# Token mixing's first layer: four groups of 112 tokens, or three of 128 and a rest of 64

## The chip, the cores and the metric

The kernel runs on one core of one Trainium2 chip. The metric is the device time of one execution in microseconds (us), as the median of several runs. The engines have short names below: PE is TensorE (its matmuls; PEld its weight loads), DVE is VectorE, ACT is ScalarE, POOL is GpSimd, and SP is SyncE, which here only issues DMAs.

## The reference

Attention with normalised queries and keys over 8 batches, 12 heads, 448 tokens and 64 columns a head; then an MLP mixer on the heads side by side, 448 tokens by 768 channels. All is float32, and the four mixer weights arrive as float64.

```python
q_n, k_n = rmsnorm(q, g_q), rmsnorm(k, g_k)
attn = softmax(q_n @ k_n.T / 8)
x = (attn @ v), heads side by side             # (8, 448, 768)
xt = x.transpose(0, 2, 1)                       # (8, 768, 448)
h = maximum(xt @ w_tok1, 0) @ w_tok2            # w_tok1 (448, 256), w_tok2 (256, 448)
u = x + h.transpose(0, 2, 1)
h2 = maximum(u @ w_ch1, 0) @ w_ch2              # w_ch1 (768, 1536), w_ch2 (1536, 768)
out = u + h2
```

What changes is the product `xt @ w_tok1`: a contraction over 448 tokens into 256 outputs, for each of 768 channels.

## The kernel before, in words

**Order of the work.** The program is one list of items per batch, which the code makes by hand: `merge` weaves lists by their given costs, `run` emits them, and `later` puts off an item (a DMA, mostly) by a number of these costed microseconds. Each engine then runs its own instructions in the order of emission. All engines but SP are scheduled by hand, and nearly all DMAs go through SP's one queue. [...]

**Attention** keeps `uT`, the attention's result with channels on partitions and tokens along the row, six tiles of 128 channels a batch. Its matmuls (`score`, L381; `values`, L454; `ones`, L434) work on 64 rows and 64 columns each, four of them on the four quarters of the array. The attention of batch b+1 is placed between the mixer's products of batch b. Queries and keys come by L1253 (`loads`), are squared on ACT (L1272), summed on DVE (L1286), folded on ACT (L1294) and made into roots from L1303 on.

**Token mixing's first layer** (`tok1`, L749) needs the tokens on partitions, so `uT` is turned first. In batch 0, `trans_x` does it with PE: four transposes a tile into one PSUM tile (L733), which ACT copies to `x` (L735). In later batches DVE transposes blocks of 32 (L741) into `xt`, four DMAs write that to DRAM (`send_x`, L709), and one DMA reads it back as `x` (`load_x`, L716): 112 partitions, each with three channel tiles by four token groups of 128 channels. The two halves h of the channels (384 each) are turned and loaded separately. `tok1(b, jc, h)` then does, for output tile jc and half h, four matmuls over groups of 112 tokens (L755) into one bank of `ps_M`, and ACT's Relu (L758) writes `h1`. A batch has four such items, (jc, h) = (0,0), (1,0), (0,1), (1,1). A float32 matmul stands in the trace as two passes.

**What follows it.** `tok2` (L763) contracts `h1` with `w_tok2`, into `ps_M` again, and DVE adds the result to `uT` (L768). `ps_M` has two banks, shared by all mixer products; `ps_S` has four, for scores, transposes and row sums. The channel mixing is a Strassen-like scheme of seven products: `ch1` (L879) and `ch2` (L936), with sums on DVE and POOL (L884, L945 and others), and weights in units that SP loads ahead from DRAM (L810). In batch 0 the natural products are done instead (`first_stage`, L851), while the weights are converted from float64 by DVE and ACT (L268 to L302) from raw loads (L176) and stored (L192). POOL then makes further sums of the weights (L204 to L207), stored by L211 and reloaded by L240, through batches 0 and 1. `trans_y` (L972) and `send_y` (L699) turn and write out the finished tiles.

**Weights of this layer.** `weight_chunks` (L133) loads `w_tok1` as two chunks of 112 rows with two token groups each, into `w1_sb`.

## Time and profile before

| | us |
|---|---|
| median of 3 runs (lowest, highest) | 1310.11 (1308.59, 1312.26) |
| the profiled execution | 1311.39 |
| its span, first to last instruction | 1309.6 |
| L755 MATMUL, 256 passes, busy | 84.5 |
| L763 MATMUL, 192 passes, busy | 78.3 |
| L879 and L936 MATMUL, 3528 passes, busy | 692.8 |
| x loads (L716): 14 DMAs of 672 KB, issue to landing | 6.9 |
| unit loads (L810): 294 DMAs of 384 KB, issue to landing | 4.1 |
| granted TensorE clock, mean | 0.994 |

A line of groups reads: line, engine, operation, tiles written and read, rows and columns of the array, shapes and count; then busy time, mean of one, and the engine's idle time ahead of it. Matmuls overlap, so a group's busy time says more than count times mean, and the spacing of starts says most. In a timeline or a chain the first number is the start from the beginning of the span, the second the length. A "q" behind an engine's name is its sequencer: it waits, or issues a DMA.

### The profile page before, as it was taken

What the parts mean: (1) busy time and instruction counts of PE and PEld (TensorE: products, weight loads), DVE (VectorE), ACT (ScalarE), POOL (GpSimd) and SP (SyncE); (2) the same over time, 40 slices, a digit from 0 to 9 for tenths busy, and PEclk for the clock granted to TensorE, in tenths of its full rate; (3) what the DMA queues carried; (4) which work ended last, traced back from release to release, by engine and by line L of the source; (5) the groups of instructions that cost most, each with busy time, mean ns of one, the idle gap of its engine ahead of it and who ended that gap; (6) DMA issues with size and microseconds to landing.
All of it is one profiled execution on the core that took longest, in us unless ns stands there. A gap on an engine that the chain in (4) does not pass through costs nothing.

```text
span 1309.6 us, 20269 instructions
## 1 busy us (share of the span) xinstructions
PE 1264.2 (97%) x7408; PEld 930.7 (71%) x7408; DVE 763.4 (58%) x1205; ACT 373.5 (29%) x740; POOL 350.6 (27%) x575
## 2 busy tenths in 40 slices
PE   5998999989998999999999999999999999999996
PEld 3444444447777688796778777796788868797996
DVE  6998768827774466645765366654666266433212
ACT  5652423213331133302441044302332033200100
POOL 1302410447352122221332122321242123111220
PEclk9999999999999999999999999999999999999999
DMA  9667485899979676686649667694757864385554
GB/s 207 171 190 179 122 218 149 196 257 254 246 203 225 146 186 157 156 224 121 163 122 233 141 152 175 157 235 98 169 151 174 204 139 142 117 224 132 172 177 83
DMA packets 502450, 228.07 MB, mean 174 GB/s; under 512 B 374532, under 2 KB 464004, under 8 KB 502340
## 3 DMA queue, kind: packets, MB, share of 16 engines
q1 hardware_dynamic: 489218, 224.83, 68.9%
q10 hardware_dynamic: 12994, 1.84, 0.8%
q8 instruction: 61, 1.00, 0.3%
q14 instruction: 49, 0.40, 0.1%
q0 software_dynamic: 128, 0.00, 0.0%
HBM read 187.07 MB, written 39.52 MB: 173 GB/s over the span
## 4 chain that ended last, share of the span: by engine, by line
PE 79%; DVE 9%; DMA 4%; SPq 3%; issue 2%; ACT 1%; POOL 1%; DVEq 0%; ACTq 0%; POOLq 0%
PE m_ps L936 25%; PE m_ps L879 25%; PE s_ps L381 8%; PE o_ps L454 8%; PE m_ps L763 5%; PE m_ps L755 5%; PE m_ps L851 3%; DVE raw L269 1%; DVE raw L271 1%; PE d_ps L434 1%; DMA qk_t<-in_k_dram 1%; DMA raw<-in_moe_w_ch_dram 1%; DVE stage L302 1%; DVE ms L1286 1%; DMA hb<-in_q_dram 1%
## 5 line engine op out<-in xcount | busy, mean ns | idle before, releaser
L936 PE MATMUL m_ps<-hb,unit 128*128 128x224 f32 x1764 | 339.8, 353 | 4.1 <-DVE uT L945 2.4
L936 PEld LDWEIGHTS m_ps<-hb,unit 128*128 128x128 f32 x1764 | 332.2, 190 | 15.2 <-issue 12.5
L879 PE MATMUL m_ps<-tu,unit 128*128 128x224 f32 x1008 | 201.9, 355 | 0.1
L879 PEld LDWEIGHTS m_ps<-tu,unit 128*128 128x128 f32 x1008 | 189.0, 190 | 14.6 <-issue 9.9
L385 ACT ACTIVATE e<-s_ps 128x448 f32<-128x448 f32 x294 | 138.3, 551 | 205.6 <-PE s_ps L381 197.5
L879 PE MATMUL m_ps<-uT,unit 128*128 128x224 f32 x756 | 151.1, 354 | 0.0
L879 PEld LDWEIGHTS m_ps<-uT,unit 128*128 128x128 f32 x756 | 142.2, 190 | 7.0 <-issue 4.6
L381 PE MATMUL s_ps<-qkT 64*64 64x448 f32 x1260 | 142.2, 545 | 0.4 <-ACT x L735 0.4
L454 PE MATMUL o_ps<-e,v 64*64 64x448 f32 x1148 | 129.1, 538 | 0.2
L422 DVE TENSOR_TENSOR es<-es,e 128x896 f32<-128x896 f32 x90 | 109.7, 1219 | 14.1 <-ACT e L385 8.9
L945 POOL TENSOR_TENSOR uT<-uT,r 128x448 f32<-128x448 f32 (+1 forms) x56 | 56.6, 1020 | 228.3 <-DVE r L945 140.9
L884 DVE TENSOR_TENSOR r<-m_ps,r 128x448 f32<-128x448 f32 x63 | 39.2, 622 | 108.1 <-PE m_ps L879 55.7
L945 DVE TENSOR_TENSOR uT<-uT,m_ps 128x448 f32<-128x448 f32 (+1 forms) x70 | 33.8, 499 | 110.9 <-PE m_ps L936 110.9
L381 PEld LDWEIGHTS s_ps<-qkT 64*64 64x64 f32 x1260 | 44.8, 132 | 67.1 <-issue 59.2
L454 PEld LDWEIGHTS o_ps<-e,v 64*64 64x64 f32 x1148 | 45.2, 133 | 62.4 <-issue 58.0
L884 POOL TENSOR_TENSOR hb<-r,r 128x448 f32<-128x448 f32 x21 | 24.0, 1145 | 235.6 <-ACT r L900 235.6
L763 PE MATMUL m_ps<-w_sb,h 128*128 128x448 f32 x192 | 78.3, 561 | 8.9 <-DVE uT L768 8.9
L755 PE MATMUL m_ps<-x,w_sb 112*128 112x384 f32 x256 | 84.5, 487 | 1.0 <-ACT x L735 1.0
L755 PEld LDWEIGHTS m_ps<-x,w_sb 112*128 112x128 f32 x256 | 48.4, 190 | 34.3 <-ACT x L735 1.3
L763 PEld LDWEIGHTS m_ps<-w_sb,h 128*128 128x128 f32 x192 | 36.5, 195 | 46.8 <-issue 27.8
L885 ACT ACTIVATE hb<-hb 128x448 f32<-128x448 f32 x63 | 36.3, 577 | 116.7 <-DVE hb L884 98.1
L1286 DVE TENSOR_REDUCE ms<-sq 128x28 f32<-128x896 f32 (+2 forms) x44 | 47.5, 1079 | 35.2 <-ACT sq L1272 32.2
(122 smaller groups left out, 1372.8 us busy)
## 6 DMA issues: line engine op xcount, KB each, us to landing
unit<-ws SPq DMA_DIRECT2D x294, 384.0 KB, 4.1
raw<-in_moe_w_ch_dram SPq DMA_DIRECT2D x72, 256.0 KB, 3.6
v<-in_v_dram SPq DMA_DIRECT2D x96, 112.0 KB, 3.7
xs<-xt SPq DMA_DIRECT2D x56, 168.0 KB, 4.7
x<-xs SPq DMA_DIRECT2D x14, 672.0 KB, 6.9
out_dram<-turned SPq DMA_DIRECT2D x168, 56.0 KB, 2.0
qk_t<-in_q_dram SPq DMA_DIRECT2D x144, 56.0 KB, 3.3
qk_t<-in_k_dram SPq DMA_DIRECT2D x144, 56.0 KB, 3.9
```

What stands on the lines that cost most here:

```text
L381: nc.tensor.matmul(out=pss[i][rows_of(i, a), 0:S], lhsT=qkT[h, 1, k * D:(k + 1) * D], rhs=qkT[h, 0, :], start=True, stop=True)
L385: nc.scalar.activation(out=e[:, i, :], in_=pss[i][:, 0:S], func=AF.Exp)
L422: nc.vector.tensor_tensor(out=es[:], in0=(es if k > 1 else st["e", t, 0])[:], in1=st["e", t, k][:], op=ALU.add)
L454: nc.tensor.matmul(out=st["o", p][a * D:(a + 1) * D, 0:S], lhsT=vt[rows, k * D:(k + 1) * D], rhs=e[rows, :], **kw)
L755: nc.tensor.matmul(out=ps[:, 0:HC], lhsT=w1_sb[0:R, c, jc * P:(jc + 1) * P], rhs=st["x", b, h][0:R, :, c, :], start=(c == 0), stop=(c == N ...
L763: nc.tensor.matmul(out=ps[:, 0:S], lhsT=st["h1", jc][:, cc * P:(cc + 1) * P], rhs=w2_sb[:, jc].rearrange("p c r -> p (c r)"), start=(jc == ...
L851: nc.tensor.matmul(out=ps, lhsT=a[:, o + 2 * half, :], rhs=natural(half)[:, :, t, :] if wide else u[:, half * KC + t, :], start=(t == 0 an ...
L879: nc.tensor.matmul(out=ps[:, j * HS:(j + 1) * HS], lhsT=w[:, t, j, :], rhs=m, start=(t == 0), stop=(t == KC - 1))
L884: add = lambda e, o, x, y: e.tensor_tensor(out=o, in0=x, in1=y, op=ALU.add)
L936: nc.tensor.matmul(out=ps[:, j * HS:(j + 1) * HS], lhsT=st["w"](j, t), rhs=hb[:, HB[what], t, :], start=(t == 0), stop=(t == KF - 1))
L945: add = lambda e, o, x, y: e.tensor_tensor(out=o, in0=x, in1=y, op=ALU.add)
L1286: self.nc.vector.tensor_reduce(out=st["ms", p][:, p % 2, lo:hi], in_=sq[:, lo:hi], axis=AX_X, op=ALU.add)
```

## The change

The 448 tokens are taken as three groups of 128 and a rest of 64. The rest is kept twice, on the lower and on the upper 64 partitions, in `x` and in `w1_sb`; the matmul of output tile 0 takes it from the lower half and that of tile 1 from the upper. In batch 0 the rest of a half follows the first tile's three groups. In later batches (`alone`) both output tiles' three groups of half 0 come first, then the four rest matmuls of both halves in one run, then half 1's three groups for each tile; half 0's two sums stay in `ps_M` until then, and half 1's two lie in `ps_S`. The Relu is moved to `tok1_out`. `load_x` issues five DMAs instead of one (three of 128 partitions, two of 64), the second chunk of `w_tok1` three instead of one, and `trans_x` three ACT copies a tile instead of one. The order of everything else on each engine is as before. `NM` is 3 and `D` is 64.

```diff
-        for c in range(0, NS, 2):
-            first.append((R, [w1v[:, c:c + 2, :]], w1_sb[0:R, c:c + 2, :].rearrange("p c n -> p (c n)")))
+        w1v = moe_w_tok1[0:2 * P].rearrange("(c p) n -> p c n", p=P)
+        rest = moe_w_tok1[NM * P:S]
+        for c, srcs in ((0, [w1v]), (2, [moe_w_tok1[2 * P:NM * P], (rest, rest)])):
+            first.append((P, srcs, w1_sb[:, c:c + 2, :].rearrange("p c n -> p (c n)")))
...
     def load_x(b, half):
-        nc.sync.dma_start(
-            out=x_tile(b, half)[0:R].rearrange("p j c n -> p (j c) n"),
-            in_=st.pop("xs")[:].rearrange("(g p) n -> p g n", p=R))
+        x, xs = x_tile(b, half), st.pop("xs")[:].rearrange("(j s) n -> s j n", j=KC)
+        for j in range(KC):
+            nc.sync.dma_start(
+                out=x[:, j, 0:NM, :], in_=xs[0:NM * P, j].rearrange("(c p) n -> p c n", p=P))
+        for a in range(2):
+            nc.sync.dma_start(out=x[a * D:(a + 1) * D, :, NM, :], in_=xs[NM * P:S])
...
-            for c in range(NS):
+            for c in range(NM):
                 nc.tensor.transpose(
-                    ps[0:R, c * P:(c + 1) * P], st["uT", b][:, j, c * R:(c + 1) * R], ident[:, :])
-            nc.scalar.copy(
-                out=st["x", b, half][0:R, o], in_=ps[0:R, :].rearrange("p (c n) -> p c n", c=NS))
+                    ps[:, c * P:(c + 1) * P], st["uT", b][:, j, c * P:(c + 1) * P], ident[:, :])
+            nc.tensor.transpose(ps[0:D, NM * P:NS * P], st["uT", b][:, j, NM * P:S], ident[:, :])
+            x = st["x", b, half]
+            nc.scalar.copy(out=x[:, o, 0:NM], in_=ps[:, 0:NM * P].rearrange("p (c n) -> p c n", c=NM))
+            for a in range(2):
+                nc.scalar.copy(out=x[a * D:(a + 1) * D, o, NM], in_=ps[0:D, NM * P:NS * P])
...
     def tok1(b, jc, h):
-        cs = slice(h * HC, (h + 1) * HC)
-        if h == 0:
-            st["h1", jc] = h1_pool.tile([P, C], F32, name="h1", tag="h1")
-        ps = m_tile()
-        for c in range(NS):
-            nc.tensor.matmul(
-                out=ps[:, 0:HC], lhsT=w1_sb[0:R, c, jc * P:(jc + 1) * P], rhs=st["x", b, h][0:R, :, c, :],
-                start=(c == 0), stop=(c == NS - 1))
-        nc.scalar.activation(out=st["h1", jc][:, cs], in_=ps[:, 0:HC], func=AF.Relu)
+
+        def main(start, stop):
+            for c in range(NM):
+                nc.tensor.matmul(
+                    out=st["t1", h][jc][:, 0:HC], lhsT=w1_sb[:, c, jc * P:(jc + 1) * P],
+                    rhs=st["x", b, h][:, :, c, :], start=start and c == 0, stop=stop and c == NM - 1)
+
+        def rest(h, starts):
+            for i in range(NJ):
+                rows = slice(i * D, (i + 1) * D)
+                nc.tensor.matmul(
+                    out=st["t1", h][i][:, 0:HC], lhsT=w1_sb[rows, NM, i * P:(i + 1) * P],
+                    rhs=st["x", b, h][rows, :, NM, :], start=starts[i], stop=not starts[i])
+
+        alone, first = b > 0 and not shifted, jc == 0
+        if first and not (alone and h):
+            st["t1", h] = [m_tile() for i in range(NJ)]
+        if not alone:
+            main(first, not first)
+            if first:
+                rest(h, (False, True))
+            tok1_out(jc, h)
+            return
+        if h == 0:
+            main(True, False)
+            return
+        if first:
+            st["t1", h] = [s_tile("t1_ps") for i in range(NJ)]
+            rest(0, (False, False))
+            rest(1, (True, True))
+            for i in range(NJ):
+                tok1_out(i, 0)
+        main(False, True)
+        tok1_out(jc, h)
+
+    def tok1_out(jc, h):
+
         if h == 0:
             st["h1", jc] = h1_pool.tile([P, C], F32, name="h1", tag="h1")
+        nc.scalar.activation(
+            out=st["h1", jc][:, h * HC:(h + 1) * HC], in_=st["t1", h][jc][:, 0:HC], func=AF.Relu)
```

More of the change, by code (lines that the diff above doesn't have):

```diff
@@ L73, in whole @@
     assert S == NK * D and NPAIR % 2 == 0 and D % 32 == 0
+    NM = S // P
+    assert S - NM * P == D and NM == NS - 1 and NJ == 2
     UNITS = 8
@@ L135, in weight_chunks @@
         first, second = [], []
-        w1v = moe_w_tok1.rearrange("(c p) n -> p c n", c=NS)
-        for c in range(0, NS, 2):
-            first.append((R, [w1v[:, c:c + 2, :]], w1_sb[0:R, c:c + 2, :].rearrange("p c n -> p (c n)")))
+        w1v = moe_w_tok1[0:2 * P].rearrange("(c p) n -> p c n", p=P)
+        rest = moe_w_tok1[NM * P:S]
+        for c, srcs in ((0, [w1v]), (2, [moe_w_tok1[2 * P:NM * P], (rest, rest)])):
+            first.append((P, srcs, w1_sb[:, c:c + 2, :].rearrange("p c n -> p (c n)")))
         for j in range(NJ):
@@ L154, in columns @@
     def columns(i):
-        src = chunks[i][1][0]
-        return WCOLS if chunks[i][2] is None or len(src.shape) == 3 else src.shape[-1]
+        return WCOLS if chunks[i][2] is None else chunks[i][2].shape[-1]
     def raw_tile():
@@ L171, in weight_load @@
             to = flat[:, k * n:(k + 1) * n]
-            if wide:
-                src = src.bitcast(U32)
-            if len(src.shape) == 3:
-                to = to.rearrange("p (i n) -> p i n", i=src.shape[1])
-            nc.sync.dma_start(out=to, in_=src)
+            for a, part in enumerate(src if isinstance(src, tuple) else (src,)):
+                at = to[a * D:(a + 1) * D] if isinstance(src, tuple) else to
+                if wide:
+                    part = part.bitcast(U32)
+                if len(part.shape) == 3:
+                    at = at.rearrange("p (i n) -> p i n", i=part.shape[1])
+                nc.sync.dma_start(out=at, in_=part)
         st["raw", i] = t
```

## The prediction

> **What bounds the kernel now.** I read the page first. It gives the span and how busy each engine is. The slices of TensorE then say where it is not busy.

> ```profile
> span 1309.6 us, 20269 instructions
> ...
> PE 1264.2 (97%) x7408; PEld 930.7 (71%) x7408; DVE 763.4 (58%) x1205; ACT 373.5 (29%) x740; POOL 350.6 (27%) x575
> ...
> PE   5998999989998999999999999999999999999996
> ```

> TensorE (PE) is the bound, but not everywhere: the digits below 9 lie in the first third. The table by stretch separates the batches (bounds, length, then busy time of PE, PEld, DVE, ACT, POOL, granted clock, DMA share):

> ```profile
> 125.00:265.60 140.60, 136.00 (x541) 63.59 (x540) 107.62 (x173) 45.66 (x82) 36.75 (x60) 0.99 0.71 177
> 265.60:431.70 166.10, 157.14 (x938) 118.50 (x937) 99.88 (x162) 46.18 (x97) 79.27 (x132) 0.99 0.91 237
> 431.70:582.70 151.00, 150.99 (x922) 118.48 (x921) 87.19 (x131) 42.35 (x87) 38.60 (x62) 1.00 0.71 173
> 582.70:733.70 151.00, 150.99 (x922) 118.49 (x921) 87.17 (x131) 42.48 (x87) 38.58 (x62) 1.00 0.69 167
> ```

> From 431.7 us on (batches 2 to 7) PE is busy in 150.99 of 151.00 us: every nanosecond taken from PE there is taken from the end. Batch 1 (265.6 to 431.7) leaves PE idle for 9.0 us, with the DMA engines 91% busy; batch 0 idles too. The waits of PE (total, times, longest) say on what, and the chain that ended last, cut to 170 to 284 us, says what stood behind it:

> ```profile
> PE m_ps L763 <- DVE uT L768: 8.9, 3, 4.8
> ...
> PE m_ps L936 <- DVE uT L945: 2.4, 1, 2.4
> PE m_ps L936 <- DMA unit<-ws: 1.7, 1, 1.7
> ```

> ```profile
> 262.47 0.80 SPq L716
> 263.27 0.05 issue
> 263.32 6.61 DMA ws<-raw
> ...
> 280.46 2.18 POOL uT L861 x2
> ```

> The stall of 4.75 us at 283.87 (inside L763) hangs on a chain SP, DMA, POOL, DVE, and the x load of L716 stands in that chain. The one of 2.37 us at 413.72 goes back, through DVE, ACT and the k load landing at 409.47, to SP's issue of that load at 405.88; SP issues without a real pause from the x load at 394.53 to there.

> Last, the stage that changes, in the timeline of PE (start, length, then the group), in batch 7 and, for what follows it, in batch 6:

> ```profile
> 1184.22 10.48 PE L755 MATMUL m_ps<-x,w_sb 112*128 112x384 f32 x32
> 1194.54 9.28 PE L763 MATMUL m_ps<-w_sb,h 128*128 128x448 f32 x24
> 1203.66 0.54 PE L879 MATMUL m_ps<-uT,unit 128*128 128x224 f32 x2
> ```

> ```profile
> 1046.03 9.29 PE L763 MATMUL m_ps<-w_sb,h 128*128 128x448 f32 x24
> 1055.25 1.73 PE L381 MATMUL s_ps<-qkT 64*64 64x448 f32 x16
> ```

> L755 takes 1194.54 - 1184.22 = 10.32 us for 32 records, two passes for each of 16 matmuls: 0.3225 us a pass, no idle. The same holds in batches 1 to 7.

> **The change, part by part.** *Matmuls, batches 1 to 7.* 16 matmuls become 12 of full height and 4 of 64 rows, two by two on opposite halves. If a pair overlaps, it takes one matmul's time: 24 + 4 = 28 passes for 32, 28 x 0.3225 = 9.03 us. That removes 1.29 us.

> *The switch of the array's tiling.* Each run of half-height matmuls now has a switch in and out. The trace shows it at the attention's 64*64 blocks. L763 takes 9.22 us (1046.03 to 1055.25) when such a block follows and 9.12 (1194.54 to 1203.66) when a full one does: 0.10. The block's own first step adds 0.05 (its records' starts lie 0.426 us apart, later ones 0.376), and after a block the first full matmul starts 0.09 later than its columns account for. Sum 0.24. The weights are now 128 columns wide (a load of 190 ns, against 132 ns for L381), which may show once more: up to 0.30. I take 0.26, so 1.29 - 0.26 = 1.03 us a batch. That four half-height matmuls stand in one run makes it one switch a batch.

> *Do the two halves overlap?* In the built program both passes of one matmul stand before the next matmul. [...] The trace speaks against it: L381's 16 records start in four bunches of four, all first passes within 0.02 us and the second passes 0.38 to 0.43 later, so eight matmuls last 1.56 us. Two of the four tiles share their columns and differ in rows alone, as the new pairs do, and write other banks. I go by the trace.

> *Batch 0.* The two halves are done in two runs: 32 passes become 28, with two switches, one of them next to an attention block that already switches: about -0.8. But PE waits for DVE at 107.95 and 112.73 (1.6 and 2.6 us, the other two of the three waits for L768 above), and DVE's conversions are independent of token mixing, so this gain is swallowed there. The transposes stay four a tile. The copy of 588 ns (L735) becomes one of 384 columns and two of 128. By ACT's other copies (235 ns for 56 columns, 345 for 224, 588 for 512) that is about 0.47 + 2 x 0.27 = 1.0: +0.4 each, 2.5 us of ACT in all, ahead of score tiles that PE waited 0.4 us for at 91.4. Below zero it can't fall except by the shorter first copy; above, +1.2 if PE had no later wait. The waits at 108 and 112 take it: 0.1.

> *Weights.* Two more SP issues near 17 us, about 0.6 us each. What DVE does at 22.5 waits for POOL, and its conversions follow until 112: 0 to 0.5, taken as 0.1.

> *The x loads.* One DMA of 672 KB becomes three of 192 and two of 96 KB: 768 KB, four more issues. An issue takes 0.32 us and 0.04 between: 4 x 0.36 = 1.46 us of SP a load. [...] And SP's next DMA behind an x load now takes about 1.1 us where 0.45 is usual, at 226.2, 263.3 and 394.9; part of the new issues goes into time that SP loses anyway. So a load costs between 0.6 us (96/672 of the 4.0 to 4.3 us that its data take in the queue) and 1.5 us. I take the middle where it lies on the path:
> - x of batch 1, first half (225.74): the raw loads and conversions of batch 0 stand behind it, with 0.7 us of slack at 228: +0.4.
> - Second half (262.47): in the chain quoted. ws<-raw at 263.32 lands right behind x: +0.9 on the stall at 283.87. This stall is not set by PE, so batch 1's 1.03 us is lost in it.
> - x of batch 2, first half (394.53): SP then issues the q and k loads: +1.1 on the stall at 413.72.
> - Second half (429.90): by the semaphores it lands at 435.96 and is needed at 436.83. Afterwards it lands near 436.7 and is needed after 12 passes, the switch and one pair, 431.67 + 3.87 + 0.12 + 0.65 = 436.3: a wait of 0.4, so batch 2 gains 0.6.
> - Batches 3 to 7: second halves land 4.8 to 6.5 us ahead of their use, first halves 19 us. SP waits there 40 us a batch for units that PE frees. No cost.

> *Buffers.* The first half's two sums hold both ps_M buffers until after the run. Their former owners are read by 1036.37 where token mixing starts at 1035.71; the second is wanted 1.94 us in. Second-half sums move to ps_S, idle there. No cost, and L763's first buffer comes free earlier, which nobody waits for.

> Sum: batches 3 to 7 -5 x 1.03 = -5.15; batch 2 -0.6; batches 0 and 1 +0.1 + 0.1 + 0.4 + 0.9 + 1.1 = +2.6. Together -3.1. The profiled execution took 1311.39 us (span 1309.6 and 1.8 around it), 1.3 above the median of 1310.11, so 1308.3 for it and 1307.0 for the median.

> **Rivals.** *The early loads are hidden:* SP's present loss of about 0.6 us after every x load absorbs the issues. Batches 2 to 7 give 6 x 1.03 = 6.2, batch 0 up to 0.9 more: 1303.0 to 1304. For: those long issues. Against: x stands in the chain. [...] *No overlap:* 32 passes and the switches, 8 x 0.26 + 2.6: 1314.8; L381 speaks against it. *SP decides (slower):* in 225 to 431 us four loads bring 16 more issues. If each delays PE by its slot of 0.36 us, that is 5.8 us, all that the steady batches and batch 2 gain; from there on the change loses. [...] For: the DMA share of 0.91. [...]

> **How the numbers follow.** Likeliest case 52% (about 1304.5 to 1309.5), early loads hidden 22%, half overlap 8%, SP decides 13%, no overlap 5%. A measurement of this kernel tells about 0.3% from no change, 3.9 us. Below 1306.2 lie the hidden case and a third of the likeliest: 0.38. Above 1314.0 lie half of SP's case and no overlap: 0.12. The rest is 0.50. The range from 1303.0 (nothing lost early) to 1312.5 (early cost of some 8 us) leaves out the lower edge of one case and the upper of two, 19% in all.

> **What would show it.** L755's stage should take 9.3 us where it took 10.32, with pairs starting within 0.02 us; batches 3 to 7 should last 149.97 us for 151.00. The stall in L763 at 284 should be longer by batch 1's gain and the chain's delay, about 6.7 us, and that at 414 about 3.5. I would be wrong if pairs don't start together, if L755 waits for x from batch 3 on, or if the stall at 414 grows by over 2 us.

## The result, and the profile after

The changed kernel takes 1307.19 us (median of 11 runs, 1303.80 to 1308.76), the kernel before, run beside it, 1310.03 (11 runs, 1307.91 to 1312.26). The ratio is 0.9974, with a 95% interval of 0.9963 to 0.9986: 2.8 us less (1.8 to 4.8 by the interval), a small gain but one that the interval keeps apart from no change. The prediction was 1307.0, within 0.3% of before as the likeliest outcome. The profiled execution took 1308.48 us, with a span of 1306.6.

In the changed file the lines move: token mixing's first layer is now L764 (groups of 128) and L771 (the rests), `tok2` L806 with DVE's addition L811, the channel mixing L922 and L979 with DVE's additions L927 and L988, the x loads L723 and L726, the writes of `xs` L714, the unit loads L853.

The table by stretch, batch 1 and then batches 2 and 3 (columns as in the table of the prediction):

```profile
265.07:434.67 169.60, 159.12 (x938) 120.45 (x937) 99.78 (x162) 46.18 (x97) 79.36 (x132) 0.96 0.92 234
434.67:584.78 150.11, 150.10 (x922) 117.58 (x921) 87.17 (x131) 42.38 (x87) 38.67 (x62) 1.00 0.72 173
584.78:734.89 150.11, 150.10 (x922) 117.57 (x920) 87.17 (x131) 42.33 (x87) 38.69 (x62) 1.00 0.69 167
```

From batch 2 on a batch is 0.90 us shorter (150.11 for 151.01), with PE as full as before. Batch 1 is longer (169.60 for 166.10 us) and PE's granted clock lower there (0.96 for 0.99). PE's waits show the same:

```profile
PE m_ps L806 <- DVE uT L811: 10.3, 3, 6.2
PE m_ps L979 <- DVE uT L988: 4.3, 1, 4.3
```

The stall in `tok2` of batch 1 has gone from 4.75 to 6.2 us, the one in `ch2` from 2.37 to 4.30, and the wait of 1.7 us for a unit is no longer there. The stage that was changed, in PE's timeline in batch 6:

```profile
1035.11 4.03 PE L764 MATMUL m_ps<-x,w_sb 128*128 128x384 f32 x12
1039.07 0.92 PE L771 MATMUL m_ps<-x,w_sb 64*128 64x384 f32 x4
1039.82 0.81 PE L771 MATMUL t_ps<-x,w_sb 64*128 64x384 f32 x4
1040.56 4.14 PE L764 MATMUL t_ps<-x,w_sb 128*128 128x384 f32 x12
1044.54 0.54 PE L806 MATMUL m_ps<-w_sb,h 128*128 128x448 f32 x1
```

1044.54 - 1035.11 = 9.43 us for 10.32. The records of L771 start in pairs (1039.073 and 1039.080, 1039.500 and 1039.506, and so on): the two halves of the array run together. This stretch, from the first L764 to the first L806, is called the stage below; the period is the time from one batch's stage to the next one's. Sorting all matmuls of both traces by their order and subtracting their starts gives where the span went: at the end of the stall of 284 us the changed kernel is 0.3 us behind, at the end of the stall in `ch2` 2.2 us (415.92 for 413.72), at the start of batch 2 3.0 (434.67 for 431.67), and at the last matmul 2.4 ahead. After that, the output's last transfers take 9.84 us for 10.44, which makes 3.0.

### The profile page after: what moved, and what is told of

The parts are those of the page before. It is cut to its first block, busy times and chain, and to the rows that moved or that the text cites. A ratio compares the mean times of both kernels' runs of the same rounds, so it can differ in the third digit from the quotient of the medians.

```text
span 1306.6 us, 20357 instructions
## 1 busy us (share of the span) xinstructions
PE 1260.9 (97%) x7408; PEld 927.2 (71%) x7408; DVE 763.7 (58%) x1205; ACT 375.9 (29%) x752; POOL 351.3 (27%) x575
## 2 busy tenths in 40 slices
PE   5998999989998999999999999999999999999996
## 4 chain that ended last, share of the span: by engine, by line
PE 83%; DVE 6%; DMA 4%; SPq 2%; issue 2%; POOL 2%; ACT 1%; DVEq 0%; ACTq 0%; POOLq 0%
PE m_ps L922 26%; PE m_ps L979 25%; PE s_ps L386 9%; PE o_ps L459 8%; PE m_ps L806 5%; PE m_ps L764 2%; PE t_ps L764 2%; PE m_ps L894 2%; DMA raw<-in_moe_w_ch_dram 1%; PE d_ps L439 1%; DVE raw L274 1%; DVE raw L276 1%; PE m_ps L439 1%; DMA hb<-in_q_dram 1%; DVE es L427 1%
## 5 line engine op out<-in xcount | busy, mean ns | idle before, releaser
L979 PE MATMUL m_ps<-hb,unit 128*128 128x224 f32 x1764 | 342.3, 355 | 4.3 <-DVE uT L988 4.3
L979 PEld LDWEIGHTS m_ps<-hb,unit 128*128 128x128 f32 x1764 | 334.5, 191 | 15.6 <-issue 10.5
L922 PE MATMUL m_ps<-tu,unit 128*128 128x224 f32 x1008 | 201.7, 355 | 0.0
L922 PEld LDWEIGHTS m_ps<-tu,unit 128*128 128x128 f32 x1008 | 189.1, 190 | 14.1 <-issue 9.2
L922 PE MATMUL m_ps<-uT,unit 128*128 128x224 f32 x756 | 151.0, 354 | 0.0
L922 PEld LDWEIGHTS m_ps<-uT,unit 128*128 128x128 f32 x756 | 142.3, 190 | 6.7 <-issue 5.3
L988 POOL TENSOR_TENSOR uT<-uT,r 128x448 f32<-128x448 f32 (+1 forms) x56 | 56.6, 1022 | 229.0 <-DVE r L988 138.5
L927 DVE TENSOR_TENSOR r<-m_ps,r 128x448 f32<-128x448 f32 x63 | 39.2, 622 | 108.0 <-PE m_ps L922 55.8
L988 DVE TENSOR_TENSOR uT<-uT,m_ps 128x448 f32<-128x448 f32 (+1 forms) x70 | 33.7, 498 | 114.2 <-PE m_ps L979 114.2
L806 PE MATMUL m_ps<-w_sb,h 128*128 128x448 f32 x192 | 78.1, 560 | 10.3 <-DVE uT L811 10.3
L927 POOL TENSOR_TENSOR hb<-r,r 128x448 f32<-128x448 f32 x21 | 24.1, 1147 | 235.8 <-ACT r L943 227.2
L806 PEld LDWEIGHTS m_ps<-w_sb,h 128*128 128x128 f32 x192 | 36.6, 195 | 48.0 <-issue 27.3
L348 DVE TENSOR_TENSOR qk_t<-qk_t,rs 128x896 f32<-128x896 f32 (+1 forms) x42 | 54.2, 1327 | 15.5 <-POOL rs L1362 15.3
L811 DVE TENSOR_TENSOR uT<-uT,m_ps 128x448 f32<-128x448 f32 x48 | 29.2, 613 | 54.2 <-PE m_ps L806 54.0
```

Source lines behind the costliest of these rows:

```text
L348: nc.vector.tensor_tensor(out=x, in0=x, in1=r.unsqueeze(2).to_broadcast(list(x.shape)), op=ALU.mult)
L806: nc.tensor.matmul(out=ps[:, 0:S], lhsT=st["h1", jc][:, cc * P:(cc + 1) * P], rhs=w2_sb[:, jc].rearrange("p c r -> p (c r)"), start=(jc == ...
L922: nc.tensor.matmul(out=ps[:, j * HS:(j + 1) * HS], lhsT=w[:, t, j, :], rhs=m, start=(t == 0), stop=(t == KC - 1))
L927: add = lambda e, o, x, y: e.tensor_tensor(out=o, in0=x, in1=y, op=ALU.add)
L979: nc.tensor.matmul(out=ps[:, j * HS:(j + 1) * HS], lhsT=st["w"](j, t), rhs=hb[:, HB[what], t, :], start=(t == 0), stop=(t == KF - 1))
L988: add = lambda e, o, x, y: e.tensor_tensor(out=o, in0=x, in1=y, op=ALU.add)
```

## The experiments

The theory: PE gains 0.90 us in each of the six batches 2 to 7, because two products on opposite row halves take one product's time, less 0.40 us for going into half-row products and out again; and four more issues a load on SP's queue give back about 3 us in batch 1, in part through a half clock behind a longer stall. The rivals are named in each expectation. In this series the kernel before took 1311.47 us (31 runs), 1.4 above its figure in the expectations, so the ratios and the profiles are to be compared, not the plain times.

**The issues alone**, in the kernel before:

```diff
-        nc.sync.dma_start(
-            out=x_tile(b, half)[0:R].rearrange("p j c n -> p (j c) n"),
-            in_=st.pop("xs")[:].rearrange("(g p) n -> p g n", p=R))
+        x = x_tile(b, half)[0:R].rearrange("p j c n -> p (j c) n")
+        xs = st.pop("xs")[:].rearrange("(g p) n -> p g n", p=R)
+        for lo, hi in ((0, 3), (3, 5), (5, 7), (7, 9), (9, 12)):
+            nc.sync.dma_start(out=x[:, lo:hi], in_=xs[:, lo:hi])
```

> The kernel before, with the load of x cut into five DMAs of the same 512-byte rows (three of 2 or 3 groups more than one): the issues of the change alone, none of its matmuls. Theory (the early loss of the change is made by the four added issues per load on SP's queue): the period of batches 2 to 6 stays at 151.0 us, the stalls at 284 and 414 us grow from 4.75 and 2.37 us towards the 6.2 and 4.3 us of the changed kernel, and the time is 1311 to 1315 us. Rival (the early loss is made by batch 0's added copies on ScalarE or by the other order of products): both stalls stay within 0.5 us of the kernel before, and the time is within 1 us of 1310.

It took 1312.30 us (12 runs), 1.0003 of before, 0.9995 to 1.0012: +0.4 us, between -0.7 and +1.6. The profile shows what the theory says, and the time little of it. PE's timeline around the stall in `ch2`, in the kernel before (start, length, group, idle ahead of it in brackets):

```profile
413.72 4.81 PE L936 MATMUL m_ps<-hb,unit 128*128 128x224 f32 x24 [2.37 <-DVE uT L945]
420.24 11.59 PE L936 MATMUL m_ps<-hb,unit 128*128 128x224 f32 x60 [1.72 <-DMA unit<-ws]
431.67 4.68 PE L755 MATMUL m_ps<-x,w_sb 112*128 112x384 f32 x14
```

with the split load:

```profile
414.89 18.94 PE L937 MATMUL m_ps<-hb,unit 128*128 128x224 f32 x84 [3.85 <-DVE uT L946]
433.67 2.75 PE L756 MATMUL m_ps<-x,w_sb 112*128 112x384 f32 x8
```

and with the change:

```profile
415.92 18.91 PE L979 MATMUL m_ps<-hb,unit 128*128 128x224 f32 x84 [4.30 <-DVE uT L988]
434.67 1.78 PE L764 MATMUL m_ps<-x,w_sb 128*128 128x384 f32 x5
```

The batch's period is 151.01 us, as before; the stalls are 5.73 and 3.85 us, most of the way to the changed kernel's 6.18 and 4.30; the one wait for a unit is gone here too; and batch 2 starts 2.0 us later than before. The two single executions differ by 1.3 us in span, inside the interval of the times. So the issues alone bring the changed shape of this stretch, though the stall's end comes 1.17 us later than before where the change makes it 2.20, and what they cost over many runs is at most 1.6 us, less than the theory's 2 to 3. Of the rival, the time came true (within 1 us of before) and the stalls did not.

**The overlap**: both tiles take the rest from the same row half.

```diff
-                rows = slice(i * D, (i + 1) * D)
+                rows = slice(0, D)
```

> The changed kernel, with both tiles of outputs taking their rest from the lower 64 rows (the same numbers lie on both halves). Theory (the stage is shorter because two products on different row halves run at once): each pair takes two steps of 0.645 us for one, the stage goes from 9.43 to 10.7 us, the period from 150.1 to 151.4, and the time is 1315 to 1319 us. Rival (the stage is shorter for another reason, as the fuller groups of 128 rows and their weight loads): the stage stays at 9.4 to 9.6 us and the time near 1307.

It took 1316.53 us (8 runs), 1.0040 of before (1.0024 to 1.0055). PE's timeline of the stage in batch 6:

```profile
1040.69 4.03 PE L764 MATMUL m_ps<-x,w_sb 128*128 128x384 f32 x12
1044.65 1.55 PE L771 MATMUL m_ps<-x,w_sb 64*128 64x384 f32 x4
1046.05 1.45 PE L771 MATMUL t_ps<-x,w_sb 64*128 64x384 f32 x4
1047.43 4.14 PE L764 MATMUL t_ps<-x,w_sb 128*128 128x384 f32 x12
1051.40 0.54 PE L806 MATMUL m_ps<-w_sb,h 128*128 128x448 f32 x1
```

10.71 us (1051.40 - 1040.69): four of L771's records now last 1.55 and 1.45 us, where they lasted 0.92 and 0.81. The overlap is worth 1.28 us a batch, four passes of 0.32, and the rival falls. Without it the change is slower than the kernel before, by its switches and by what it loses in batch 1.

**The switch**: two runs of half-row products in a batch for one.

```diff
             rest(0, (False, False))
-            rest(1, (True, True))
             for i in range(NJ):
                 tok1_out(i, 0)
-        main(False, True)
+        main(first, not first)
+        if first:
+            rest(1, (False, True))
```

> The changed kernel, with the two halves' rests not one behind the other but with three full products between them, so that TensorE goes into the half-row products and out of them twice in a batch. Theory (each entry and exit costs 0.40 us in all, four steps of 0.427 us or 0.41 us instead of 0.32 us): the stage goes from 9.43 to 9.83 us, the period from 150.1 to 150.5, and the time to 1309.5 to 1310.5 us. Rival (what looks like the price of a switch is paid once for each stage, by the first step of new weights or by a slow start of the stage): the stage stays within 0.1 us of 9.43.

It took 1310.72 us (12 runs), 0.9998 of before (0.9987 to 1.0009). The stage:

```profile
1034.81 4.03 PE L764 MATMUL m_ps<-x,w_sb 128*128 128x384 f32 x12
1038.77 0.92 PE L771 MATMUL m_ps<-x,w_sb 64*128 64x384 f32 x4
1039.62 2.20 PE L764 MATMUL t_ps<-x,w_sb 128*128 128x384 f32 x6
1041.75 0.92 PE L771 MATMUL t_ps<-x,w_sb 64*128 64x384 f32 x4
1042.59 2.20 PE L764 MATMUL t_ps<-x,w_sb 128*128 128x384 f32 x6
1044.63 0.54 PE L807 MATMUL m_ps<-w_sb,h 128*128 128x448 f32 x1
```

9.82 us (1044.63 - 1034.81), 0.39 more for the second entry and exit, and 0.40 x 7 batches = 2.8 us is about what the time lost against the change ((0.9998 - 0.9974) x 1310 = 3.1). The price belongs to the switch, not to the stage.

**The clock**: PE kept at work in the stall.

```diff
         put_off_done()
+        if b == 1 and group == 1 and i == 0:
+            ps = s_tile("warm")
+            for k in range(4):
+                nc.tensor.matmul(
+                    out=ps[:, 0:HC], lhsT=w1_sb[:, 0, 0:P], rhs=w2_sb[:, 0].rearrange("p c r -> p (c r)")[:, 0:HC],
+                    start=True, stop=True)
         n = 2 - group
```

> The changed kernel, with four products of 128x384 into a spare bank, whose result nobody reads, ahead of the product that waits at 414 us (about 2.6 us of TensorE's work inside a stall of 4.3 us). Theory (the half clock from 414.7 us on follows from TensorE's standing still for 4.3 us): the granted clock stays full there, the passes behind the stall take 0.19 us and not 0.37 us, and the time is 1304 to 1305.5 us. Rival (the half clock comes from something else at that place, as load or a clock of its own): the passes from 416 to 421 us still take 0.37 us and the time is 1307 us or more.

It took 1307.91 us (12 runs), 0.9973 of before (0.9960 to 0.9985): no gain over the change (the two intervals leave some 2 us either way), where the theory wanted 1.7 to 3.2 us. Yet the clock did what it said. The stretch from 411 to 436 us (bounds, length, busy times, granted clock, DMA share), with the change and then with the products in the stall:

```profile
411.00:436.00 25.00, 20.70 (x93) 19.32 (x92) 8.97 (x19) 2.24 (x6) 5.98 (x16) 0.86 0.91 240
```

```profile
411.00:436.00 25.00, 20.81 (x99) 18.34 (x98) 8.97 (x19) 2.23 (x6) 5.91 (x16) 1.00 0.90 238
```

The mean clock is 1.00 for 0.86, and the passes behind the stall start 0.19 us apart for 0.37. PE's timeline says where the gain went:

```profile
410.43 2.74 PE L970 MATMUL warm<-w_sb 128*128 128x384 f32 x8
415.29 4.81 PE L985 MATMUL m_ps<-hb,unit 128*128 128x224 f32 x24 [2.11 <-DVE uT L994]
422.17 11.59 PE L985 MATMUL m_ps<-hb,unit 128*128 128x224 f32 x60 [2.08 <-DMA unit<-ws]
433.60 2.74 PE L764 MATMUL m_ps<-x,w_sb 128*128 128x384 f32 x8
```

The wait for a unit, which the change had seemed to remove, is back with 2.08 us. SP's queue there, with the products in the stall, shows why:

```profile
410.66 1.75 SPq L216 DMA_DIRECT2D ws<-raw  x2
416.86 0.32 SPq L714 DMA_DIRECT2D xs<-xt  x1
417.36 1.78 SPq L853 DMA_DIRECT2D unit<-ws  x3
```

The unit is issued behind a write of `xs`, which waits for DVE's transposes, and these stand behind the same DVE addition that ends PE's stall. So it is issued 2.07 or 2.08 us after the stall's end in all three kernels (413.72 and 415.79 before, 415.92 and 418.00 with the change, 415.29 and 417.36 here); it lands 4.31 us later before and 4.67 here. PE at half clock comes to the products that need it at 423.32, 5.32 us after the issue, and does not wait; at full clock it would be there 4.6 us after the stall's end (24 passes, 0.19 us apart), before the landing, and waits. The half clock is real, but its cost is mostly cover for that wait: from the stall's end to batch 2 it is 17.95 us before, 18.75 with the change, 18.31 here. The rival (a clock that has nothing to do with the stall) falls, and so does the theory's price.

## Why the prediction was right, step by step

**The overlap** was right. The halves run at once, as L381 had shown, and the program order of the passes holds nothing up: the pair's first passes start 7 ns apart and the second passes 0.43 us later, again 6 ns apart. In the program both passes of one product stand before the next product, and still the second product's first pass starts 0.42 us ahead of the first product's second pass. No run shows what the half overlap among the chances of the prediction supposes. Removing the overlap costs 1.28 us a batch, where 1.29 was worked out.

**The switch** was mis-sized: "I take 0.26", with 0.30 as the upper bound, against 0.40 measured. The starts of the full rate lie 0.323 us apart; around the run they lie 0.416 (the last full pass to the first pair), 0.427 (the first pair to the second), 0.419 (the last pair to the first full pass) and 0.427 us (the first full pass to its second). The excesses are 0.093, 0.104, 0.096 and 0.104, 0.397 in all. The sum in the prediction counted three places, with 0.05 for the second, where the weights are narrower; it missed the fourth, the first step after the exit. That one could be read in the trace of before: behind the attention block that ends at 457.38, the first two passes of L879 start 0.294 us apart, the later ones 0.189. So a steady batch gains 0.90 us and not 1.03.

**Batch 2** did not lose the 0.4 us put down to its second x load: its stage took 9.43 us as the others, so it gained the full 0.90. The load's first issue comes 2.2 us later than before (432.09 for 429.90), but the batch starts 3.0 us later. The steady part, 6 x 0.90 = 5.4 us, came out near the predicted 5.15 + 0.6 = 5.75.

**Batch 0 and the first x load** had 0.6 us of loss in the sum (0.1, 0.1 and 0.4). One execution can't show that: batch 1 starts at 265.07 us for 265.62, half a microsecond early, and between 262.85 and 265.89 in the six traces.

**The issues** were mis-sized too: 1.46 us for four more (by the prediction's own 0.36 each, 1.44). From the first issue of x to SP's next DMA it is 2.77 us in batch 3 (560.19 to 562.96) for 0.37 (558.19 to 558.56), so 2.40 for four more, and at 394.69 it is 3.62 for 0.36, so 3.26. What was right is that a good part of it goes into time that SP lost before. The five are under way together: where the landings are recorded, the last of them lands 5.6 to 7.2 us after the first issue, and the one DMA of before 6.1 to 7.7 us after its own. Nor does a run show a cost of an issue that would put half of SP's case above 1314.0 us, as the chances have it: with the split load alone the time was 1.0003 of before (0.9995 to 1.0012).

**The stall at 284 us** was to grow "by batch 1's gain and the chain's delay", to about 6.7 us; it is 6.18 us, and ends at 284.18 for 283.87, only 0.3 us later. That small shift flatters the chain, for SP came to the x load in it 0.41 us earlier (262.06 for 262.47). Counted from that issue, the stall ends 21.40 us later before and 22.12 with the change, 0.72 more, and 21.58 to 22.42 in the other four kernels with five issues; the prediction had +0.9. The `ws<-raw` behind the load are issued 2.55 us later (265.87 for 263.32), but the reloads `raw<-ws`, for which POOL waits, only 0.15 later (273.40 for 273.25). By the stall in `ch2` the changed kernel stands 0.3 us behind (PE falls idle at 411.62 for 411.35).

**The stall at 414 us** was under-sized: +1.1 predicted, +1.93 measured in length and +2.20 in its end, just short of the 2 us of growth that the prediction named as a sign of being wrong. SP's queue around the x load, before:

```profile
394.53 0.31 SPq L716 DMA_DIRECT2D x<-xs  x1
394.89 1.15 SPq L1253 DMA_DIRECT2D qk_t<-in_q_dram  x1
396.08 3.19 SPq L1253 DMA_DIRECT2D qk_t<-in_k_dram  x4
...
405.88 0.45 SPq L1253 DMA_DIRECT2D qk_t<-in_k_dram  x1
```

and with the change:

```profile
394.69 2.29 SPq L723 DMA_DIRECT2D x<-xs  x3
397.03 1.24 SPq L726 DMA_DIRECT2D x<-xs  x2
398.31 0.60 SPq L1296 DMA_DIRECT2D qk_t<-in_q_dram  x1
398.95 2.04 SPq L1296 DMA_DIRECT2D qk_t<-in_k_dram  x4
...
407.32 0.45 SPq L1296 DMA_DIRECT2D qk_t<-in_k_dram  x1
```

The first q load is issued 3.42 us later, but behind it the long issues of before (1.15 us, and four of 0.86 to 0.98 among the q and k loads) are gone now but for one of 1.05, much as the prediction said, and at the last k load 1.44 us of delay are left, the upper end of its 0.6 to 1.5. That load then took 4.36 us to land, 0.77 more than the 3.59 of before, which no term had. 1.44 + 0.77 = 2.21 is the 2.20 by which the stall ends later. With the split load in the kernel before, the same two terms are 0.93 and 0.14 (issued at 406.81, landed in 3.73), together 1.07 of the 1.17.

**The half clock** was not foreseen. From 414.71 us on, still inside the stall of 4.30 us, PE is granted half its clock for 6.83 us. Its price is not the 2.7 us that its slow passes lost: the wait for the unit, 1.72 us, vanishes under it, and 18.75 - 17.95 = 0.8 us is left. Against the kernel with PE kept at work it is 0.44 (18.75 - 18.31). Nor does it belong to the change alone: the mean granted clock was 0.994 in the profiled execution of before, but its median over the 31 runs of the experiments is 0.991, against 0.992 in the 11 runs of the change. Worked out from these means (0.003 of 1310 us, twice), a middling run of before stands an estimated 8 us longer at half clock than the one that was profiled; the rounding of the means leaves 5 to 10.

The sum in the profiled executions: -5.4 us for six batches, +3.0 up to batch 2 (0.3 before the stall, 1.9 in it, 0.8 behind it), -0.6 in the last transfers, together -3.0, against -3.1 predicted. So the total was right partly by luck: the steady gain came out smaller by 0.3 and the early loss larger by 0.4, and the profile's total is met only with a tail that no step spoke of. The tail is 9.7 to 10.4 us in the six profiles, and both ends are in kernels with the same instructions there (10.44 before, 9.72 with the split load), so its 0.6 counts as scatter.

**What stays open.** Over many runs the issues alone cost 0.4 us (-0.7 to +1.6), but the steady gain of 5.4 less the measured 2.8 leaves 2.6 for the early part (0.6 to 3.6 by the interval of the ratio). The intervals meet, so the issues may be all of it. But the change also brings 96 KB more a load, three ACT copies a tile in batch 0 and two more issues for `w_tok1`, which were not run by themselves, and one profile a kernel can't part them, since batch 2's start scatters: it is 434.67, 435.11, 432.75 and 433.60 us in the four kernels with the new loads. Counted from the moment PE falls idle ahead of the stall in `ch2`, it is 20.3 us before and 22.3 to 23.2 in all five kernels with five issues (the one with PE kept at work counted from where its extra products begin), so in these executions that place is a loss of 2 to 3 us in each. Over many runs the split load costs less than that, which fits the finding above that a middling run of before has more half clock than the profiled one; that this is the reason is not shown, nor where in the run the half clock falls. A detour of x with longer rows and three issues a load, which would tell issues from packets, was not tried, and no version here beats the change.

## What to carry to other kernels

A gain in a stage counts where that stage's engine is full, and the queue that feeds it has to be read in the stages where it is not: here six full batches kept 0.9 us each, and a stretch with idle time took about half of it back, in part at least through four more issues a load. When an engine waits twice in a row, ask whether the second wait hangs on the end of the first; if so, speeding up what lies between them can lengthen the second, as the wait for a unit came back here with 2.08 us. Count a change of the array's tiling at both ends, the entry and the exit, two steps each (0.40 us in all here), and put all such products in one run (a second run cost 0.39 us).

## What the runs showed of the hardware

```profile
409.92:413.34 3.42, 1.43 (x8) 1.08 (x6) 1.70 (x4) 1.51 (x5) 0.13 (x1) 1.00 1.30 227
413.34:416.75 3.41, 3.03 (x16) 3.04 (x17) 2.43 (x5) 0.34 (x1) 2.68 (x10) 1.00 0.29 66
219.19:222.60 3.41, 1.38 (x5) 0.80 (x5) 3.31 (x6) 2.84 (x5) 1.34 (x1) 1.00 1.05 228
222.60:226.01 3.41, 3.41 (x6) 1.41 (x5) 3.38 (x3) 0.76 (x1) 1.45 (x2) 0.50 0.86 222
283.63:287.04 3.41, 3.17 (x5) 1.53 (x6) 1.55 (x4) 0.00 (x0) 3.25 (x8) 0.50 1.08 378
287.04:290.45 3.41, 3.41 (x11) 1.74 (x10) 2.19 (x5) 0.00 (x0) 2.35 (x5) 1.00 1.01 399
413.02:416.43 3.41, 2.64 (x7) 2.43 (x8) 2.83 (x6) 0.00 (x0) 2.49 (x9) 0.50 0.24 66
416.43:419.85 3.42, 3.42 (x10) 3.10 (x10) 0.00 (x0) 0.34 (x1) 1.52 (x5) 0.50 0.94 210
```

- In the traces of before and of the change, from about 20 us to the last products, the 7 steps at full clock with 2.21 us idle or more were followed by half clock, and none with 1.99 us or less was; with the split load one with 2.03 us was (3.41 - 1.38, the third row). The 7 steps at half clock with up to 0.44 us idle were followed by full clock, and the two with 1.21 and 2.59 us by another at half, as was one with 0.77 us with two runs (3.41 - 2.64, the seventh row). A stall's length alone did not tell: the 2.37 us up to 413.72 in the kernel before lay in two steps, with 1.99 and 0.38 us, and brought no half clock, while 2.21 us up to 222.38 with the change lay in one step and brought 3.41 us of it. The stall of 4.75 us in the kernel before ended 0.24 us into the half step and brought 3.41 us at half; that of 3.38 us with two runs reached 0.77 us into it and brought 6.83.
